# Softmax of the strided heads in batches 0 and 1: one subtraction on VectorE, one exponential, one sum, and batch 1's mask from TensorE

## The chip, the cores and the metric

The kernel runs on one core of a Trainium2 chip. The metric is the device time of one execution in microseconds (us); lower is better. Five engines work side by side, each on its own queue in order: TensorE (PE in the profile; PEld is its weight load), VectorE (DVE), ScalarE (ACT), GpSimd (POOL) and SyncE (SP), which here issues every DMA.

## What is computed

Three stages follow one another: sparse attention, a gated feed-forward, and a soft mixture of experts.

```python
# q, k, v: (4 batches, 8 heads, 576 positions, 64)
scores = scale * np.matmul(q, k.transpose(0, 1, 3, 2))
mask_local = (rel >= 0) & (rel < 32)                             # heads 0 to 3
mask_strided = (rel >= 0) & (pos[None, :] % 32 == pos[:, None] % 32)   # heads 4 to 7
scores = np.where(masks, scores, -1e9)
scores = scores - np.max(scores, axis=-1, keepdims=True)
attn = np.exp(scores)
attn = attn / (np.sum(attn, axis=-1, keepdims=True) + 1e-09)
x = np.matmul(attn, v)                  # then (2304 tokens, 512)
h = x @ w_in                            # 512 -> 2048
x = (h / (1 + np.exp(-1.702 * h))) @ w_out
logits = x @ phi                        # 32 slots; softmax over tokens and over slots,
...                                     # 8 experts on 4 slots each, and the mix back
```

## The kernel before

**Attention.** Heads go in pairs: pairs 0 and 1 are local, pairs 2 and 3 strided. A strided pair has its positions sorted by residue, so its scores become 11 units of 64 query rows x 64 keys (18 positions of each of three residues, hence a block mask). Two heads stand side by side on 128 partitions. The 11 units are split into part 0 (6 units, 384 elements per partition) and part 1 (5 units, 320 elements), each in one PSUM tile `s`. `att_scores` computes them (L176). For batch 0 it first writes the mask into the tile by a bf16 product of the identity `identb` and `maskb` (L166), and the scores accumulate on top. For the other batches VectorE adds the mask later, while it moves the scaled scores from `s` into the SBUF tile `ts` (L192).

**Softmax.** `att_softmax` takes a part at a time. VectorE finds the negated maximum of each unit's rows (L202); in batch 0 it also scales this (L204). ScalarE then runs one exponential per unit (L207): the bias is that unit's negated maximum, and the sum along the row comes out through the accumulator, which shows as a second instruction, ACTIVATION_READ_ACCUMULATOR. VectorE adds 1e-9 and takes the reciprocal (L208, L209). GpSimd multiplies (L210). After that `att_transpose` turns the probabilities on TensorE (L225) and copies them out (L227, L229), and `att_values` multiplies by v (L244) and splits the result into two rounded tiles `x` (L269 on ScalarE, L270 on VectorE).

**The order.** Batch 0 runs alone at the start; `keep_busy` puts filler products on TensorE between its steps (L87). Then the feed-forward runs over five chunks of tokens (c) and sixteen column blocks (f) each; a step (c, f) is one `gemm1`: twelve products (L353), a tanh on ScalarE (L356) and a gate on VectorE (L357). Chunk 0 carries batch 1's attention beside it, chunk 1 batch 2's, chunk 2 batch 3's. Chunk 0 also converts the raw weights: two ScalarE and two VectorE instructions for each block of 512 columns (`narrow`: L286, L287, L288, L289, tiles `wc`, `wt`, `neg`), then a rounded part on ScalarE (L306) and the remainder on GpSimd (L307). The `wt` tiles feed the small products `wp` (L314). The instruction order on each engine is laid out at build time by the framework's planner, from its own estimates of costs; only the last stage is ordered by hand. The PSUM tiles of attention come from a pool of five.

Of the kernel before, what the change touches and what calls it, by code (L numbers as in the profile page):

```python
# [9 lines left out]
F32 = mybir.dt.float32  # L10
# [6 lines left out]
AF = mybir.ActivationFunctionType  # L17
ALU = mybir.AluOpType
AX = mybir.AxisListType
# [12 lines left out]
SCALE = 0.125  # L32
# [16 lines left out]
def tile_kernel(ctx: ExitStack, tc: tile.TileContext, lqk, lv, sqk, sv, wraw, phi, wexp, cst, out):  # L49
    nc = tc.nc  # L50
    P = 128
# [14 lines left out]
    att = att_es.enter_context(tc.tile_pool(name="att", bufs=2, side="right"))  # L66
# [7 lines left out]
    def mtile(name):  # L74
        return ps_m.tile([P, 512], F32, tag="m", name=name)
# [67 lines left out]
    def att_units(hp):  # L143
        local = hp < 2
        return (KL, QT, S, NTL, 5, maskL) if local else (KS, QS, SW, NTS, HS, maskS)

    def att_scores(b, hp, parts=(0, 1)):
        t = qkv[b, hp]
        local = hp < 2
        nk, step, ko, total, half, mask = att_units(hp)  # L150
        early = b == 0
        shape = [P, NTL if local else 2 * HS, nk]
        if (b, hp) not in probs:
            if b == 0 and hp >= 2:
                ts = ep.tile(shape, F32, name=f"ts_{b}_{hp}")
            else:
                ts = att.tile(shape, F32, tag="ts", name=f"ts_{b}_{hp}")
            probs[b, hp] = ts
            if not local:
                nc.gpsimd.memset(ts[:, NTS], 0.0)  # L160
        sp = sps.setdefault((b, hp), {})
        for part in parts:
            nt = (half, total - half)[part]
            sp[part] = (mtile(f"s_{b}_{hp}_{part}")[:, :nt * nk].rearrange("p (u k) -> p u k", k=nk))
            if early:
                nc.tensor.matmul(sp[part], identb, mask.unsqueeze(1).to_broadcast([P, nt, nk]), start=True, stop=False)  # L166
                if local and part == 0:
                    nc.tensor.matmul(sp[0][:, 0], identb, maskL0, start=False, stop=False)
        for u in range(half):
            for part in parts:  # L170
                if part * half + u >= total:
                    continue
                qo = step * (part * half + u)
                for h in range(2):
                    hs, o = slice(64 * h, 64 * h + 64), 64 * (h ^ part)
                    nc.tensor.matmul(sp[part][o:o + 64, u], t[hs, qo:qo + 64], t[hs, ko + qo:ko + qo + nk], start=not early, stop=not early or part * half + u in (half - 1, total - 1))  # L176

    def att_softmax(b, hp, part):
        local = hp < 2
        nk, step, ko, total, half, mask = att_units(hp)  # L180
        u0, u1 = (0, half) if part == 0 else (half, total)
        nt = u1 - u0
        early = b == 0
        nm = f"{b}_{hp}_{part}"
        sp = sps[b, hp][part]
        if local:
            ts = probs[b, hp][:, u0:u1]
        else:
            ts = probs[b, hp].rearrange("p (j e) k -> p e j k", e=2)[:, part, :nt]

        def add_mask(a, z, m):
            nc.vector.scalar_tensor_tensor(ts[:, a:z], sp[:, a:z], SCALE, m.unsqueeze(1).to_broadcast([P, z - a, nk]), op0=ALU.mult, op1=ALU.add)  # L192

        if not early:
            if local and part == 0:
                add_mask(0, 1, maskL0)
                add_mask(1, nt, mask)
            else:
                add_mask(0, nt, mask)
        nmx = att.tile([P, 6], F32, tag="nmx", name=f"nmx_{nm}", bufs=4)  # L200
        src, sc = (sp, SCALE) if early else (ts, 1.0)
        nc.vector.tensor_reduce(nmx[:, :nt], src, axis=AX.X, op=ALU.max, negate=True)  # L202
        if early:
            nc.vector.tensor_scalar_mul(nmx[:, :nt], nmx[:, :nt], SCALE)  # L204
        sm = att.tile([P, 6], F32, tag="sm", name=f"sm_{nm}", bufs=4)
        for u in range(nt):
            nc.scalar.activation(ts[:, u], src[:, u], AF.Exp, scale=sc, bias=nmx[:, u:u + 1], accum_out=sm[:, u:u + 1])  # L207
        nc.vector.tensor_scalar_add(sm[:, :nt], sm[:, :nt], 1e-9)  # L208
        nc.vector.reciprocal(sm[:, :nt], sm[:, :nt])  # L209
        nc.gpsimd.tensor_tensor(ts, ts, sm[:, :nt].unsqueeze(2).to_broadcast([P, nt, nk]), op=ALU.mult)  # L210

    def att_transpose(b, hp):
        ts = probs.pop((b, hp))
# [394 lines left out]
    def attention_units(b):  # L608
        la = 2 if b else 4
        order = list(range(la)) + [x for u in range(la, 8) for x in (la - 1 - u, u)] + list(range(la - 9, -9, -1))  # L610
        for x in order:
            if x >= 0:
                if b and x % 2 == 0:
                    load_qk(b, x // 2)
                att_scores(b, x // 2, (x % 2,))
                att_softmax(b, x // 2, x % 2)
                if b == 0:
                    keep_busy(1)
            else:
                x = -x - 1  # L620
                if x % 2:
                    att_values(b, x // 2)
                else:
                    if b:
                        load_v(b, x // 2)
                    att_transpose(b, x // 2)
                    if (b, x) == (1, 6):
                        load_qk(2, 0)
                if b == 0:
                    keep_busy(4)  # L630
            yield

    def attention_pairs(b):
        for hp in range(4):
            if hp:
                att_values(b, hp - 1)
            att_scores(b, hp)
            att_softmax(b, hp, 0)
            yield
            att_softmax(b, hp, 1)  # L640
            load_v(b, hp)
            if hp < 3:
                load_qk(b, hp + 1)
            yield
            if hp < 3:
                yield
            att_transpose(b, hp)
            yield
        att_values(b, 3)
        if b < 3:  # L650
            load_qk(b + 1, 0)
        yield
# [284 lines left out]
```

## Time and profile before

| | |
|---|---|
| median of 3 runs | 414.33 us (413.97 to 415.26) |
| profiled execution, its own time | 415.33 us |
| its span, first to last instruction | 413.5 us |
| TensorE busy | 387.9 us, 94% |
| VectorE busy | 267.6 us, 65% |
| ScalarE busy | 224.8 us, 54% |
| GpSimd busy | 52.4 us, 13% |
| mean granted TensorE clock | 0.986 |

The shares are means over stages that differ. In the forty slices of the span ScalarE is at 80% or more, mostly over 90%, through much of the first quarter and then falls away, while TensorE is at 90% or more for nearly the whole rest. The first quarter is batch 0's attention and chunk 0 with batch 1's attention, which is where all the changed code runs.

### The profile page before, as it was taken

The numbers are of one execution on the slowest core, as the hardware profiler recorded it, in microseconds if no ns is written. First come the engines' busy times: TensorE is split into PE (matmuls) and PEld (weight loads), VectorE is DVE, ScalarE is ACT, GpSimd is POOL, SyncE is SP. The second block draws the span as 40 slices with busy tenths as digits, with TensorE's granted clock in tenths as the row PEclk, the third lists the DMA queues.
The fourth block names the chain that finished last, engine by engine and source line by source line (L and its number), as shares of the span: only waits on it lengthen the run. The fifth ranks groups of instructions, "written<-read, shape, count | busy, mean of one in ns | idle before, by whom it ended". The sixth has DMA issues, their size and how long they took to land.

```text
span 413.5 us, 9788 instructions
## 1 busy us (share of the span) xinstructions
PE 387.9 (94%) x3930; PEld 269.4 (65%) x3935; DVE 267.6 (65%) x569; ACT 224.8 (54%) x668; POOL 52.4 (13%) x64
## 2 busy tenths in 40 slices
PE   8998998897999999989999999999999999799992
PEld 3656766664776657857767685776778788333682
DVE  2679887799688668868677878547454666412132
ACT  2899789998876546675854758321212222310141
POOL 0433333432310100010110101000000000010000
PEclk9999899999999999999999999999999999999997
DMA  8966477766731422546752442596002899879998
GB/s 237 390 216 212 138 229 238 226 214 229 232 128 43 165 78 98 179 164 211 265 201 78 139 170 101 207 366 268 2 0 103 313 379 334 316 292 406 419 391 259
DMA packets 27917, 89.26 MB, mean 216 GB/s; under 512 B 2400, under 2 KB 9696, under 8 KB 23776
## 3 DMA queue, kind: packets, MB, share of 16 engines
q1 hardware_dynamic: 27872, 88.64, 60.7%
q8 instruction: 31, 0.51, 0.5%
q14 instruction: 14, 0.11, 0.1%
HBM read 79.71 MB, written 8.91 MB: 214 GB/s over the span
## 4 chain that ended last, share of the span: by engine, by line
PE 64%; ACT 16%; DVE 11%; issue 3%; DMA 2%; POOL 2%; SPq 0%; ACTq 0%; DVEq 0%; POOLq 0%
PE h L353 34%; ACT ts L207 7%; PE u L479 5%; PE op L803 4%; PE hp L773 3%; PE lg L372 3%; PE ptp L225 2%; ACT neg L287 2%; PE s L176 2%; PE av L244 2%; DMA qk<-lqk 2%; DVE x L270 2%; PE fp L819 2%; ACT gT L356 2%; DVE wc L289 1%
## 5 line engine op out<-in xcount | busy, mean ns | idle before, releaser
L353 PE MATMUL h<-x,wi 128*128 128x512 f32 (+1 forms) x960 | 217.1, 378 | 2.8 <-DVE gT L357 2.6
L353 PEld LDWEIGHTS h<-x,wi 128*128 128x128 f32 x960 | 165.3, 190 | 52.0 <-issue 14.0
L356 ACT ACTIVATE gT<-h 128x512 f32<-128x512 f32 (+1 forms) x54 | 29.4, 545 | 51.6 <-PE h L353 51.6
L357 DVE SCALAR_TENSOR_TENSOR gT<-gT,h 128x512 f32<-128x512 f32 (+1 forms) x54 | 33.3, 617 | 34.7 <-ACT gT L356 34.3
L207 ACT ACTIVATE ts<-ts,nmx 128x64 f32<-128x64 f32 (+1 forms) x120 | 41.4, 348 | 11.3 <-DVE nmx L202 11.3
L210 POOL TENSOR_TENSOR ts<-ts,sm 128x384 f32<-128x384 f32 (+2 forms) x32 | 27.5, 859 | 156.8 <-DVE sm L209 75.1
L356 ACT ACTIVATE more<-h 128x512 f32<-128x512 f32 (+1 forms) x26 | 14.8, 568 | 40.6 <-PE h L353 40.6
L287 ACT ACTIVATE neg<-raw,ebias 128x512 f32<-128x512 int16 x48 | 36.6, 762 | 0.0
L380 DVE STREAM_TRANSPOSE gT<-gT 128x512 f32<-128x512 f32 (+1 forms) x54 | 34.3, 640 | 1.5 <-PE lg L372 0.3
L307 POOL TENSOR_TENSOR wi<-wc,wi 128x512 fp32r<-128x512 f32 x16 | 22.0, 1374 | 26.0 <-ACT wi L306 17.0
L357 DVE SCALAR_TENSOR_TENSOR more<-more,h 128x512 f32<-128x512 f32 (+1 forms) x26 | 16.9, 651 | 12.6 <-ACT more L356 12.0
L269 ACT CAST x<-av 128x320 fp32r<-128x320 f32 (+20 forms) x54 | 18.9, 400 | 10.9 <-DVE x L270 9.1
L225 PE MATMUL ptp<-cs,ts 128*96 128x128 f32 (+1 forms) x120 | 17.3, 279 | 6.7 <-POOL ts L210 3.7
L479 PE MATMUL u<-gT,dT 32*32 32x512 f32 x576 | 21.4, 597 | 2.0 <-DVE z L537 1.6
L207 ACT ACTIVATION_READ_ACCUMULATOR ts<-ts,nmx 128x1 f32 x120 | 22.5, 188 | 0.0
L270 DVE TENSOR_TENSOR x<-av,x 128x320 fp32r<-128x320 f32 (+20 forms) x54 | 19.9, 394 | 2.6 <-ACT x L269 2.6
L372 PE MATMUL lg<-gT,wp 128*32 128x512 f32 (+1 forms) x100 | 19.9, 566 | 1.1 <-DVE gT L357 1.1
L225 PEld LDWEIGHTS ptp<-cs,ts 128*96 128x96 f32 (+1 forms) x120 | 13.0, 133 | 11.7 <-POOL ts L210 10.5
L176 PEld LDWEIGHTS s<-qk 64*64 64x64 f32 x552 | 15.8, 136 | 5.9 <-issue 4.4
L176 PE MATMUL s<-qk 64*64 64x96 f32 (+1 forms) x552 | 18.9, 240 | 0.6 <-DMA qk<-lqk 0.6
L380 DVE STREAM_TRANSPOSE gT<-more 128x512 f32<-128x512 f32 (+1 forms) x26 | 17.3, 671 | 1.6 <-PE u L479 1.0
L244 PEld LDWEIGHTS av<-pt,v 96*64 96x64 f32 (+2 forms) x552 | 13.9, 136 | 5.8 <-issue 3.5
(154 smaller groups left out, 475.6 us busy)
## 6 DMA issues: line engine op xcount, KB each, us to landing
ex<-wexp SPq DMA_DIRECT2D x28, 1024.0 KB, 7.0
raw<-wraw SPq DMA_DIRECT2D x48, 511.8 KB, 4.0
qk<-lqk SPq DMA_DIRECT2D x8, 592.0 KB, 5.8
wo_scr<-wo SPq DMA_DIRECT2D x16, 256.0 KB, 2.3
ex<-wo_scr SPq DMA_DIRECT2D x4, 1024.0 KB, 9.8
gT<-wexp SPq DMA_DIRECT2D x4, 1024.0 KB, 6.0
qk<-sqk SPq DMA_DIRECT2D x6, 604.0 KB, 5.2
v<-lv SPq DMA_DIRECT2D x8, 432.0 KB, 5.1
```

The source lines that it names most:

```text
L176: nc.tensor.matmul(sp[part][o:o + 64, u], t[hs, qo:qo + 64], t[hs, ko + qo:ko + qo + nk], start=not early, stop=not early or part * half + ...
L207: nc.scalar.activation(ts[:, u], src[:, u], AF.Exp, scale=sc, bias=nmx[:, u:u + 1], accum_out=sm[:, u:u + 1])
L210: nc.gpsimd.tensor_tensor(ts, ts, sm[:, :nt].unsqueeze(2).to_broadcast([P, nt, nk]), op=ALU.mult)
L225: nc.tensor.transpose(ptp[:nk, u - a], src, ident)
L270: nc.vector.tensor_tensor(dsts[1], src, dsts[0].bitcast(F32), op=ALU.subtract)
L287: nc.scalar.activation(n, top, AF.Relu, scale=-(2.0 ** 19), bias=ebias)
L353: nc.tensor.matmul(h[:, :N], w[:, we, 128 * kt:128 * kt + 128], x[xe][:, kt, :N], start=n == 0, stop=n == 11)
L356: st["tanh"] = nc.scalar.activation(g[:, :N], h[:, :N], AF.Tanh, scale=0.851).ins
L357: st["gate"] = nc.vector.scalar_tensor_tensor(g[:, :N], g[:, :N], 1.0, h[:, :N], op0=ALU.add, op1=ALU.mult).ins
L372: nc.tensor.matmul(lgs[c][32 * j:32 * j + 32, :N], wp[:, f0 + j, :], gs[c, f0 + j][:, :N], start=f0 == 0, stop=f0 == NF - 4)
L380: nc.vector.transpose(t_slots(c)[:, f, :N], gs[c, f][:, :N])
L479: nc.tensor.matmul(us[a][32 * j:32 * j + 32, :].rearrange("p (t f) -> p t f", f=32), dT[q, 32 * b:32 * b + 32], gT[q, :, 32 * b:32 * b + 3 ...
```

## The change

For strided pairs of batches 0 and 1 (`joined`), the softmax of a part becomes: the negated maximum of the raw scores on VectorE; one VectorE addition of that maximum to the whole part, from PSUM into `ts`; one exponential with a constant scale over the whole part, in place; one VectorE sum over it. The end (reciprocal, GpSimd's multiplication) is as before, in a helper. For batch 1 the mask of these pairs now comes from TensorE, as in batch 0. Local pairs, and batches 2 and 3, stay as they are.

```diff
@@ att_scores
-        early = b == 0
+        early = b == 0 or b == 1 and not local
@@
+    def softmax_scale(ts, sm, nt, nk):
+        nc.vector.tensor_scalar_add(sm[:, :nt], sm[:, :nt], 1e-9)
+        nc.vector.reciprocal(sm[:, :nt], sm[:, :nt])
+        nc.gpsimd.tensor_tensor(ts, ts, sm[:, :nt].unsqueeze(2).to_broadcast([P, nt, nk]), op=ALU.mult)
@@ att_softmax
+        joined = b < 2 and not local
...
-        if not early:
+        if not early and not joined:
...
+        sm = att.tile([P, 6], F32, tag="sm", name=f"sm_{nm}", bufs=4)
+        if joined:
+            nc.vector.tensor_reduce(nmx[:, :nt], sp, axis=AX.X, op=ALU.max, negate=True)
+            nc.vector.tensor_tensor(ts, sp, nmx[:, :nt].unsqueeze(2).to_broadcast([P, nt, nk]), op=ALU.add)
+            nc.scalar.activation(ts, ts, AF.Exp, scale=SCALE)
+            nc.vector.tensor_reduce(sm[:, :nt], ts, axis=AX.X, op=ALU.add)
+            softmax_scale(ts, sm, nt, nk)
+            return
...
-        sm = att.tile([P, 6], F32, tag="sm", name=f"sm_{nm}", bufs=4)
         for u in range(nt):
             nc.scalar.activation(ts[:, u], src[:, u], AF.Exp, scale=sc, bias=nmx[:, u:u + 1], accum_out=sm[:, u:u + 1])
-        nc.vector.tensor_scalar_add(sm[:, :nt], sm[:, :nt], 1e-9)
-        nc.vector.reciprocal(sm[:, :nt], sm[:, :nt])
-        nc.gpsimd.tensor_tensor(ts, ts, sm[:, :nt].unsqueeze(2).to_broadcast([P, nt, nk]), op=ALU.mult)
+        softmax_scale(ts, sm, nt, nk)
```

## Rows read from the trace of the kernel before

**Rows 1.** Windows of the span: busy us of each engine, its instructions, clock, DMA

```profile
16.00:41.00 25.00, 22.41 (x338) 16.18 (x338) 20.66 (x52) 23.58 (x94) 8.46 (x9) 1.00 0.72 248
66.00:83.00 17.00, 15.21 (x129) 11.00 (x128) 13.20 (x25) 16.11 (x46) 6.39 (x6) 1.00 0.72 226
83.00:104.00 21.00, 18.55 (x149) 11.73 (x146) 20.37 (x36) 19.08 (x52) 5.52 (x6) 0.94 0.63 218
106.00:414.00 308.00, 294.42 (x3026) 205.14 (x3023) 185.49 (x400) 135.90 (x387) 17.30 (x25) 0.99 0.58 210
```

**Rows 2.** Chain of work that ended last, 0 to 112 us: start, us, what

```profile
17.37 1.90 ACT ts L207 x12
...
22.57 1.91 ACT ts L207 x12
...
69.46 1.51 ACT ts L207 x9
...
89.43 1.52 ACT ts L207 x9
```

**Rows 3.** TensorE's waits, 16 to 111 us: total us, times, longest

```profile
PE ptp L225 <- POOL ts L210: 2.6, 4, 1.2
PE h L353 <- DVE gT L357: 2.6, 4, 1.3
PE ptp L225 <- DVE sm L208: 2.2, 1, 2.2
PE wp L314 <- DVE wt L289: 1.9, 2, 1.7
```

**Rows 4.** ScalarE's timeline, batch 0, then batch 1: start, us, what

```profile
17.37 0.32 ACT L207 ACTIVATE ts<-s,nmx 128x64 f32<-128x64 f32 x1
...
19.12 0.35 ACT L269 CAST x<-av 128x192 fp32r<-128x192 f32 x1
...
27.86 0.50 ACT L229 COPY pt<-ptp 128x384 f32<-128x384 f32 x1
28.21 0.81 ACT L287 ACTIVATE neg<-raw,ebias 128x512 f32<-128x512 int16 x1
...
68.89 0.33 ACT L207 ACTIVATE ts<-ts,nmx 128x64 f32<-128x64 f32 x1
...
70.88 0.61 ACT L306 CAST wi<-wc 128x512 fp32r<-128x512 f32 x1
71.39 0.59 ACT L356 ACTIVATE gT<-h 128x512 f32<-128x512 f32 x1
```

**Rows 5.** VectorE's timeline: start, us, what

```profile
85.76 0.55 DVE L192 SCALAR_TENSOR_TENSOR ts<-s,maskb 128x384 f32<-128x384 f32 x1
86.22 1.52 DVE L289 SCALAR_TENSOR_TENSOR wt<-raw,wt 128x512 uint32<-128x512 uint32 x1
...
88.27 0.54 DVE L202 TENSOR_REDUCE nmx<-ts 128x6 f32<-128x384 f32 x1
88.73 0.67 DVE L288 TENSOR_TENSOR wc<-wc,neg 128x512 int32<-128x512 f32 x1
...
95.61 0.48 DVE L202 TENSOR_REDUCE nmx<-ts 128x5 f32<-128x320 f32 x1
96.01 1.78 DVE L289 SCALAR_TENSOR_TENSOR wc<-raw,wc 128x512 uint32<-128x512 uint32 x1
```

**Rows 6.** VectorE's groups by form, 0 to 112 us: busy us, mean ns

```profile
L204 DVE TENSOR_SCALAR nmx<-nmx 128x6 f32<-128x6 f32 x2 | 0.4, 220 | 0.1
```

**Rows 7.** TensorE's timeline around a mask product and two waits

```profile
15.10 0.33 PE L166 MATMUL s<-maskb,identb 128*128 128x384 bf16 x1
15.35 0.92 PE L176 MATMUL s<-qkv 64*64 64x64 f32 x24
...
41.79 0.75 PE L225 MATMUL ptp<-cs,ts 128*96 128x128 f32 x5 [2.24 <-DVE sm L208]
```

**Rows 8.** Windows of 2 us: columns as in the first group

```profile
44.00:46.00 2.00, 2.00 (x22) 1.63 (x21) 1.09 (x2) 2.00 (x4) 0.27 (x2) 0.50 0.06 12
```

## The prediction

> **What bounds the kernel now.** I read the windows of the span first, since the shares of the whole hide the stages [rows 1]. From 106 us on, TensorE is busy 294.4 of 308 us and ScalarE 135.9: that part is TensorE's own, none of the changed instructions lies in it, and what is gained or lost ahead of it should reach the end one for one. The changed code runs in three earlier stretches: 16 to 41 us (batch 0's strided pairs, then the first steps of the feed-forward) and 66 to 83 and 83 to 104 us (batch 1's strided pairs, beside the weight conversion). There the picture is another. ScalarE is busy 23.58 of 25 us, 16.11 of 17 and 19.08 of 21. VectorE stands at 20.66, 13.20 and 20.37 in the same stretches. So ScalarE is the fullest engine in the first two, and VectorE in the third, where it has only 0.63 us left.
>
> Second, the chain of waits [rows 2]. Between 16 and 104 us it runs mostly through ScalarE and VectorE, and the exponentials of the strided parts stand in it: a whole part at 17.37 and at 22.57 us (1.9 us each, twelve instructions), and most of one at 69.46 and 89.43. The reader is to see that a part's six exponentials are not hidden: the next block of weights or the next part stands behind them on ScalarE's queue.
>
> Third, TensorE's waits between 16 and 111 us [rows 3]. They sum to 2.6 + 2.6 + 2.2 + 1.9 = 9.3 us, for probabilities, for the gate, and for converted weights. That is the most that relief of the other engines could give back in this region if nothing else took over. One of them, 2.24 us ahead of 41.79, is the largest single hole [rows 7]; it ends only when the softmax of batch 1's first (local) part is through, which stands behind weight conversion on both engines.
>
> **What the change removes.** Prices are steps in the queue, from the start of the first to the start of what comes next, because consecutive instructions overlap. In batch 0 six exponentials with their accumulator reads take from 17.37 to 19.12, 1.75 us; five take 5/6 of that, 1.46. In batch 1, from SBUF, six take from 68.89 to 70.88, 1.99 us; five take 1.66 [rows 4]. The trace has no exponential over a whole part. The nearest rows bound it: the copy of 384 elements out of PSUM steps 0.35 us (27.86 to 28.21), the rounding of 512 elements in SBUF steps 0.51 (70.88 to 71.39) [rows 4]. I take 0.40 for 384 elements and 0.35 for 320; the ends would shift a part by 0.1 us at most. Each batch has two parts of each size. ScalarE's relief is
>
> - batch 0: 2 x (1.75 - 0.40) + 2 x (1.46 - 0.35) = 4.9 us
> - batch 1: 2 x (1.99 - 0.40) + 2 x (1.66 - 0.35) = 5.8 us
>
> The scaling of the negated maximum in batch 0 goes too: four instructions of some 0.2 us [rows 6], of which the queue feels perhaps 0.12 each, 0.5 us in all.
>
> **What it adds to VectorE.** The sum over a part has the shape of the maximum that is already there: 88.27 to 88.73 is 0.46 us for 384 elements, 95.61 to 96.01 is 0.40 for 320 [rows 5]. The subtraction reads PSUM and a broadcast operand and writes `ts`, as the mask addition does, which steps 0.46 us for 384 elements (85.76 to 86.22) [rows 5]; 320 elements I put at 0.40, as for the sum. The trace has no subtraction with this operand; as it has one PSUM operand of the same size, I see no reason for more than 0.1 us either way. In batch 0 both are new: 2 x (0.46 + 0.46) + 2 x (0.40 + 0.40) = 3.4 us, less the 0.5 above, so +2.9. In batch 1 the subtraction takes the mask addition's place at the same price, and only the sums are new: 2 x 0.46 + 2 x 0.40 = +1.7 us.
>
> **What it adds to TensorE.** Four mask products in batch 1. In batch 0 one of 384 columns steps 0.25 us (15.10 to 15.35) [rows 7]; four, two of them shorter, are at most 1.0 us. Below, they cost nothing where they fall into one of the waits of [rows 3], which is ahead of the scores in some places at best. I count half, 0.5 us.
>
> **What moves.** In batch 0 the PSUM tile `s` comes free after the subtraction instead of after the last exponential, well over 1 us earlier. In batch 1 it is held from the maximum through the subtraction, one more VectorE step than before, about 0.5 us plus what the planner puts between them. No transfer is added or moved. The new waits are the sum's on the exponential, and the exponential's on the subtraction. Behind the sum on VectorE's queue stand weight conversion and gates; the exponential is 0.4 us long, so the wait is short if ScalarE's queue is short, and the accumulator's reader (L208) had the same wait before. GpSimd's multiplication keeps its work. The latency of one part without queues goes from 0.1 + 1.75 (scaled maximum and exponentials, batch 0) to 0.46 + 0.40 + 0.46, some 0.5 us less.
>
> **A price against it.** The sum that ScalarE's accumulator gave inside its own instruction is now a VectorE reduction, 0.46 us in the rows of the same shape [rows 5], in a stretch where VectorE has 0.63 us left [rows 1]. The Trainium skill speaks against that: VectorE: DVE Perf Modes, section Rules for kernel authors, expects a reduction to run at the plain rate only, calls it the slowest VectorE operation, and asks to restructure one that lies on the hot path. By that rule the third stretch would lose what the sums cost; this is the second rival below, and the rows bear it out for that stretch alone.
>
> **The sum by stretches.** 16 to 41 us: ScalarE falls to 23.6 - 4.9 = 18.7 us, VectorE rises to 20.7 + 2.9 = 23.6 of 25. VectorE is next, so at most 1.4 us can go, and TensorE's queue there holds fillers in a fixed order. I take 0.8 us. Bounds: 1.4, and on the other side a loss of 0.5, if VectorE's conversions slip by one subtraction.
>
> 66 to 104 us, taken together since conversion runs steps ahead: ScalarE falls from 35.2 to 29.4, VectorE rises from 33.6 to 35.3, TensorE from 33.8 to at most 34.8, of 38 us. VectorE is again next, at most 38 - 35.3 = 2.7 us can go. VectorE was 88% busy with ScalarE nearly full beside it; if it reaches 95% with ScalarE at ease, the stretch takes 37.2 us, 0.8 less. The chain gives more: it passes 1.5 us and more of exponentials at 69.46 and at 89.43, each of which shrinks to 0.4, 2.2 us together, before VectorE takes over. Between 0.8 and 2.2 I take 1.8, less the 0.5 of mask products: 1.3 us.
>
> Together 2.1 us. The profiled execution took 415.33 us for a span of 413.5, 1.0 above the median of 414.33; the difference is applied to the median: **412.2 us**, 0.5% less. A difference of 0.3%, 1.2 us, is about what can be told from no change.
>
> **The rivals.**
>
> *ScalarE's relief is used up by the next queue* (chance 0.22). Fillers hold TensorE's order in batch 0 and VectorE follows at once. For: VectorE is at 83%, 78% and 97% in the three stretches [rows 1]. Then 0.4 us remains of the 2.1: 413.9, no change that can be told.
>
> *VectorE becomes the bound, and it is slower* (chance 0.17). Place: 83 to 104 us. The two sums of the fourth pair add 0.46 + 0.40 = 0.86 us to 20.37, 21.23 in a stretch of 21; the wait of the `wp` products for converted weights [rows 3] grows by as much, and the pair's mask products add 0.5 us. If the first stretch gives nothing either, the time is 414.3 + 0.9 + 0.5 = 415.7. It decides from the point where VectorE has no idle time left to take the sums, and where ScalarE's relief in 66 to 83 does not let conversion run ahead. Against it: in 66 to 83 VectorE has 3.8 us idle, in which earlier conversion fits.
>
> *The whole chain shrinks* (chance 0.12). Both ceilings are reached, 1.4 + 2.7 = 4.1 us: 410.2. The clock could add to it: at 44 to 46 us TensorE is granted 0.50 of full speed, the 1.2 GHz level [rows 8], after the 2.24 us hole [rows 7]; at full clock the same work would take 1 us less, if the smaller hole left the clock up. I count none of it, and let the low end hold part of it.
>
> *The change doesn't do what it says* I leave out: which instructions are issued is plain from the code; only the planner's new order is open, and it may move any of the above by about 1 us.
>
> **How the numbers follow.** Forecast 0.49 (own range 411.0 to 413.0), used up 0.22, slower 0.17, whole chain 0.12. Faster by over 0.3%: nearly all of the first and the last, 0.58. Within 0.3%: 0.25. Slower: 0.17. The range, 409.7 to 415.4, takes in the low end's 410.2 with half of the clock's 1 us, and reaches up to the slower rival short of its full price; what lies outside is some 0.15.
>
> **What would show it.** Right: ScalarE's busy time 66 to 104 us near 29, eight exponentials of 0.45 to 0.55 us each in place of 44 pairs; VectorE up by 4.6 us in the first 110; the last batch 1 strided probabilities ready before 104 us, and everything after 106 us the same, only earlier. Wrong: VectorE continuously busy from 83 us with a larger wait of `wp` for `wt`; a larger hole near 40 us; a new hole ahead of batch 1's strided scores (PSUM tile not free); or a gain at 106 us that is gone by the end.

## The result and the profile after

The changed kernel takes **410.85 us** (median of 4 runs, 410.67 to 411.28). The kernel before, run beside it on the same chip, takes 414.38 (413.97 to 415.26). The ratio is 0.9913, with an interval of 0.9896 to 0.9931: 3.5 us faster, where 2.1 us were forecast. The profiled execution took 410.86 us, with a span of 409.1. One execution of all those below, of the run with the first seven remainders on VectorE, was in a slow state, and medians and ratios leave it out.

I read the windows first, as before. These rows answer to [rows 1]; the columns are the same, and 66 to 104 us is added in one piece:

```profile
16.00:41.00 25.00, 22.05 (x331) 15.90 (x325) 23.81 (x57) 20.45 (x54) 10.14 (x9) 1.00 0.77 253
...
66.00:83.00 17.00, 17.00 (x134) 11.89 (x131) 16.75 (x30) 16.25 (x32) 9.11 (x7) 1.00 0.69 247
83.00:104.00 21.00, 19.07 (x162) 13.20 (x156) 21.00 (x39) 17.46 (x32) 7.47 (x7) 1.00 0.73 248
106.00:409.00 303.00, 289.89 (x3000) 201.57 (x2989) 183.24 (x396) 132.66 (x381) 16.03 (x24) 0.99 0.58 210
...
66.00:104.00 38.00, 36.07 (x293) 25.09 (x287) 37.75 (x68) 33.72 (x63) 16.58 (x13) 1.00 0.72 248
```

The same row of the kernel before, which the prediction formed as a sum of two:

```profile
66.00:104.00 38.00, 33.76 (x274) 22.73 (x270) 33.57 (x61) 35.20 (x97) 11.91 (x11) 0.97 0.67 221
```

The roles have changed sides. In 66 to 104 us VectorE is now the full engine, 37.75 of 38 us. ScalarE has 34 instructions fewer but is only 1.5 us less busy. Replacing 44 exponentials and accumulator reads by 4 leaves 57 of its 97 instructions; the profile shows 63, so six others have moved into the stretch from later on: four of the weight conversion, a tanh and a copy of `wpT`. TensorE does 2.3 us more in it.

The new instructions by form, 0 to 112 us (busy us, mean ns of one, idle time ahead), with the mask products' group that now holds batch 1's too:

```profile
L210 DVE TENSOR_TENSOR ts<-s,nmx 128x384 f32<-128x384 f32 x4 | 2.2, 550 | 0.0
L212 DVE TENSOR_REDUCE sm<-ts 128x6 f32<-128x384 f32 x4 | 2.2, 546 | 0.4 <-ACT x L280 0.4
L211 ACT ACTIVATE ts<-ts 128x384 f32<-128x384 f32 x4 | 2.1, 519 | 0.6 <-DVE ts L210 0.6
L166 PE MATMUL s<-maskb,identb 128*128 128x384 bf16 x6 | 2.0, 330 | 0.0
...
L212 DVE TENSOR_REDUCE sm<-ts 128x5 f32<-128x320 f32 x4 | 1.9, 482 | 0.1
L210 DVE TENSOR_TENSOR ts<-s,nmx 128x320 f32<-128x320 f32 x4 | 1.9, 480 | 0.0
L211 ACT ACTIVATE ts<-ts 128x320 f32<-128x320 f32 x4 | 1.9, 473 | 0.3 <-DVE ts L210 0.3
```

TensorE's waits, 16 to 111 us, which answer to [rows 3]:

```profile
PE ptp L236 <- DVE sm L179: 3.4, 1, 3.4
PE ptp L236 <- POOL ts L181: 3.3, 4, 1.3
PE h L364 <- DVE gT L368: 1.0, 1, 1.0
PE h L364 <- ACT wt L297: 0.2, 1, 0.2
```

They sum to 7.9 us instead of 9.3. The wait of `wp` for converted weights is gone and the gate's has shrunk from 2.6 to 1.0, but the single hole near 40 us [rows 7] has grown from 2.24 to 3.44.

To see where the time went, I took four points of TensorE's timeline that every run has: the start of batch 1's first strided scores, of its last strided scores, of batch 2's first scores, and the end. Up to batch 1's first strided scores both kernels need the same (65.23 and 65.22 us), and up to its last ones too (91.46 and 91.60). From there to batch 2's first scores it is 23.47 us before and 19.52 after. From there to the end of the span it is 298.6 and 298.0. Of the 4.4 us between the two spans, 3.95 arise in the 20 us behind the last strided scores, where feed-forward and weight conversion finish.

### The profile page after: what moved, and what is told of

It reads as the page before. It is cut to its first block, busy times and chain, and to the rows that moved or that the text cites. A ratio compares the mean times of both kernels' runs of the same rounds, so it can differ in the third digit from the quotient of the medians.

```text
span 409.1 us, 9725 instructions
## 1 busy us (share of the span) xinstructions
PE 385.8 (94%) x3939; PEld 269.3 (66%) x3939; DVE 272.5 (67%) x577; ACT 215.7 (53%) x588; POOL 55.1 (13%) x64
## 4 chain that ended last, share of the span: by engine, by line
PE 64%; DVE 16%; ACT 11%; issue 4%; DMA 2%; POOL 2%; SPq 0%; DVEq 0%; ACTq 0%; POOLq 0%
PE h L364 33%; ACT ts L220 5%; PE u L490 5%; PE op L814 4%; PE hp L784 3%; PE lg L383 3%; PE av L255 3%; PE s L176 3%; PE ptp L236 2%; DVE x L281 2%; DVE gT L368 2%; DMA qk<-lqk 2%; PE fp L830 2%; POOL ts L181 1%; DVE wc L300 1%
## 5 line engine op out<-in xcount | busy, mean ns | idle before, releaser
L368 DVE SCALAR_TENSOR_TENSOR gT<-gT,h 128x512 f32<-128x512 f32 (+1 forms) x54 | 33.2, 616 | 31.8 <-ACT gT L367 31.4
L181 POOL TENSOR_TENSOR ts<-ts,sm 128x384 f32<-128x384 f32 (+2 forms) x32 | 29.7, 929 | 148.4 <-DVE sm L180 73.1
L220 ACT ACTIVATE ts<-ts,nmx 128x96 f32<-128x96 f32 (+1 forms) x98 | 34.2, 352 | 12.4 <-DVE nmx L216 12.4
L318 POOL TENSOR_TENSOR wi<-wc,wi 128x512 fp32r<-128x512 f32 x16 | 22.2, 1388 | 26.4 <-ACT wi L317 26.2
L236 PE MATMUL ptp<-cs,ts 128*96 128x128 f32 (+1 forms) x120 | 17.4, 282 | 8.6 <-POOL ts L181 4.9
L368 DVE SCALAR_TENSOR_TENSOR more<-more,h 128x512 f32<-128x512 f32 (+1 forms) x26 | 16.9, 648 | 12.1 <-ACT more L367 11.5
L236 PEld LDWEIGHTS ptp<-cs,ts 128*96 128x96 f32 (+1 forms) x120 | 13.3, 134 | 14.2 <-POOL ts L181 13.2
L383 PE MATMUL lg<-gT,wp 128*32 128x512 f32 (+1 forms) x100 | 20.9, 566 | 0.8 <-DVE gT L368 0.8
L220 ACT ACTIVATION_READ_ACCUMULATOR ts<-ts,nmx 128x1 f32 x98 | 18.5, 189 | 0.0
L240 ACT COPY pt<-ptp 96x384 f32<-96x384 f32 (+1 forms) x34 | 14.7, 478 | 5.7 <-PE ptp L236 5.6
```

The costliest lines, as they stand in the source:

```text
L236: nc.tensor.transpose(ptp[:nk, u - a], src, ident)
L368: st["gate"] = nc.vector.scalar_tensor_tensor(g[:, :N], g[:, :N], 1.0, h[:, :N], op0=ALU.add, op1=ALU.mult).ins
L383: nc.tensor.matmul(lgs[c][32 * j:32 * j + 32, :N], wp[:, f0 + j, :], gs[c, f0 + j][:, :N], start=f0 == 0, stop=f0 == NF - 4)
```

## The experiments

Each diff is against the changed kernel. Each ratio is against the kernel before on the same chip (its medians there were 414.77 to 415.12, and 414.38 for the first row of the changed kernel). The stretches are A, span start to batch 1's first strided scores; B, to its last strided scores; C, to batch 2's first scores; each is a difference of starts in TensorE's timeline. They come from the one profiled execution of each run, which lies up to 1.2 us from its run's median and 2.2 us above it for the extra copy, so they don't add up to the differences of the medians.

| run | ratio (interval) | A | B | C |
|---|---|---|---|---|
| kernel before | 1 | 65.2 | 26.2 | 23.5 |
| changed kernel | 0.9913 (0.9896 to 0.9931) | 65.2 | 26.4 | 19.5 |
| batch 0 only | 0.9977 (0.9959 to 0.9995) | 64.5 | 25.9 | 23.5 |
| batch 1 only | 0.9967 (0.9953 to 0.9981) | 65.5 | 25.0 | 22.7 |
| mask move alone | 0.9958 (0.9938 to 0.9978) | 64.4 | 26.6 | 22.7 |
| two sums | 0.9940 (0.9919 to 0.9961) | 65.8 | 26.2 | 20.1 |
| changed kernel again | 0.9909 (0.9876 to 0.9942) | 64.3 | 26.4 | 19.6 |
| extra copy | 1.0013 (0.9984 to 1.0041) | 65.6 | 27.5 | 22.6 |
| fillers | 0.9942 (0.9921 to 0.9962) | 66.3 | 24.5 | 19.9 |
| all remainders on VectorE | 0.9918 (0.9891 to 0.9945) | 61.3 | 26.3 | 24.6 |
| first seven on VectorE | 0.9880 (0.9849 to 0.9911) | 60.9 | 27.1 | 22.8 |
| batch 1 only, last three on VectorE | 0.9969 (0.9953 to 0.9984) | 65.5 | 25.0 | 22.0 |
| batch 1 only, first seven on VectorE | 0.9867 (0.9840 to 0.9894) | 62.6 | 26.3 | 19.4 |
| batch 1 only, last three left out | 0.9912 (0.9884 to 0.9939) | 64.9 | 25.1 | 20.6 |

Stretch A also varies with the landing of the first loads: batch 0's first scores start between 6.3 and 7.5 us.

**The halves.** Batch 0 joined alone, then batch 1 alone:

```diff
-        early = b == 0 or b == 1 and not local
+        early = b == 0
...
-        joined = b < 2 and not local
+        joined = b == 0 and not local
```

> Only batch 0's strided pairs are joined; batch 1 as in the kernel before. Theory A (batch 1 carries the whole gain; in batch 0 VectorE took over and the hole near 40 us grew from 2.24 to 3.44 us): 414.0 to 415.2 us, no change or a little slower, with VectorE at about 23.8 of 25 us between 16 and 41 us. Theory B (the prediction's split, 0.8 us from batch 0): 413.0 to 413.8.

```diff
-        joined = b < 2 and not local
+        joined = b == 1 and not local
```

> Only batch 1's strided pairs are joined, with the mask from TensorE; batch 0 as before. Theory A: 410.0 to 411.2 us, the whole gain or more, with TensorE's hole near 40 us back at about 2.2 us. Theory B: 411.6 to 413.0, since batch 0's share is missing. If neither half alone gives the gain, it comes from the planner's order of the two together (theory C).

Batch 0 alone took 414.13 us, 0.23% less than before; batch 1 alone 413.61, 0.33% less. The halves add up to 0.56%; the whole gives 0.87%. By these ratios alone the difference is hardly outside the noise, since their intervals reach 0.14 to 0.18% either way. Stretch C says it more plainly: it is 0.0 and 0.7 us shorter with the halves, and 3.9 us with the whole and with its repetition. So something in stretch C hangs on both. Batch 1 alone has VectorE's work of 66 to 104 us (36.87 us busy, 33.82 for ScalarE, nearly those of the whole change) and yet loses most of C's gain. VectorE's timeline of that run ahead of the gate (L368), for which TensorE waits:

```profile
98.54 0.49 DVE L209 TENSOR_REDUCE nmx<-s 128x5 f32<-128x320 f32 x1
98.94 1.39 DVE L300 SCALAR_TENSOR_TENSOR wc<-raw,wc 128x512 uint32<-128x512 uint32 x1
100.26 0.68 DVE L299 TENSOR_TENSOR wt<-wt,neg 128x512 int32<-128x512 f32 x1
100.86 0.48 DVE L210 TENSOR_TENSOR ts<-s,nmx 128x320 f32<-128x320 f32 x1
101.26 1.63 DVE L300 SCALAR_TENSOR_TENSOR wt<-raw,wt 128x512 uint32<-128x512 uint32 x1
102.81 0.68 DVE L368 SCALAR_TENSOR_TENSOR gT<-gT,h 128x512 f32<-128x512 f32 x1
```

GpSimd's timeline of the same run:

```profile
97.93 1.86 POOL L318 TENSOR_TENSOR wi<-wc,wi 128x512 fp32r<-128x512 f32 x1 [2.89 <-DVE x L281]
101.06 1.28 POOL L318 TENSOR_TENSOR wi<-wc,wi 128x512 fp32r<-128x512 f32 x1 [1.28 <-ACT wi L317]
```

TensorE's timeline shows what follows:

```profile
103.54 2.56 PE L364 MATMUL h<-x,wi 128*128 128x512 f32 x10 [2.79 <-DVE gT L368]
```

The same six instructions of VectorE in the changed kernel:

```profile
97.43 0.48 DVE L209 TENSOR_REDUCE nmx<-s 128x5 f32<-128x320 f32 x1
97.83 0.68 DVE L300 SCALAR_TENSOR_TENSOR wc<-raw,wc 128x512 uint32<-128x512 uint32 x1
98.43 0.68 DVE L299 TENSOR_TENSOR wt<-wt,neg 128x512 int32<-128x512 f32 x1
99.03 0.48 DVE L210 TENSOR_TENSOR ts<-s,nmx 128x320 f32<-128x320 f32 x1
99.43 0.67 DVE L300 SCALAR_TENSOR_TENSOR wt<-raw,wt 128x512 uint32<-128x512 uint32 x1
100.03 0.67 DVE L368 SCALAR_TENSOR_TENSOR gT<-gT,h 128x512 f32<-128x512 f32 x1
```

From the maximum to the gate it is 2.60 us here and 4.27 us with batch 1 alone. The instructions are the same; two conversions (L300, L289 in the kernel before) take 1.39 and 1.63 us instead of 0.68, each beside one of GpSimd's remainders (L318); such a pair is called a meeting below. In the changed kernel the remainders of this time lie at 95.67 and 100.26 us, mostly beside other instructions. That became the theory for the rest: where GpSimd's two-input instructions fall decides what VectorE's conversions cost, and so what stretch C takes.

**The mask move alone.** The exponentials stay single in both batches, batch 1's mask comes from TensorE (both lines in `att_softmax`):

```diff
-        early = b == 0
-        joined = b < 2 and not local
+        early = b == 0 or b == 1 and not local
+        joined = False
```

> Batch 1's strided mask comes from TensorE, but the exponentials stay one per unit with bias and accumulator, in both batches; nothing is joined. VectorE then does a tiny scaling (0.1 us) in place of a mask addition (0.46), so it is relieved by about 1.4 us, ScalarE's exponentials from PSUM step 0.29 in place of 0.33 us, TensorE gets four mask products. Theory A (ScalarE's queue was what held the conversion back): 413.6 to 415.0, little changed. Rival (VectorE's relief and the mask products make the gain): 411 to 412.5.

Measured: 413.41 us, 0.42% less than before, a little faster than theory A said, and short of the rival. Four mask additions leave VectorE, tiny scalings take their place, and TensorE's four products cost no time that shows. The mask move alone thus gives as much as batch 1 joined with it (0.33%): in this order of instructions, joining batch 1 alone adds nothing to it.

**Two sums.** Is VectorE the bound now? Batch 1's four sums are formed twice:

```diff
             nc.vector.tensor_reduce(sm[:, :nt], ts, axis=AX.X, op=ALU.add)
+            if b:
+                extra = att.tile([P, 6], F32, tag="extra", name=f"extra_{nm}", bufs=2)
+                nc.vector.tensor_reduce(extra[:, :nt], ts, axis=AX.X, op=ALU.add)
```

> The changed kernel with each of batch 1's four sums done twice (the second into a tile nobody reads): 1.7 us more on VectorE between 66 and 104 us. If VectorE is now the bound of that stretch (it is busy 37.75 of 38 us): 1.2 to 2.0 us slower than the changed kernel, 412.0 to 412.9. If its idle time elsewhere hides them: under 0.5 us, 410.8 to 411.3.

Measured: 412.55 us, 1.1 to 1.7 us over the two medians of the changed kernel (411.43 and 410.85), for 2 x 0.46 + 2 x 0.40 = 1.7 us of added queue steps. So by the medians most of VectorE's added time counts, as the theory of a full VectorE expects. The profiled executions don't place the loss there: B and C together, where the sums stand, take 46.3 us against 45.9, and the rest of the difference lies in A and behind C, where nothing was added. In 66 to 104 us conversions longer than 0.95 us take 3.9 us more than 0.68 each would, against 5.3 in the changed kernel, which may hide 1.4 of the 1.7 us there. The run is in line with VectorE as the bound, and doesn't show it by itself.

**The changed kernel again**, as a control beside the next three:

> The changed kernel once more, unaltered, as the yardstick for the other three runs on the same chip: a ratio of 0.989 to 0.993 to the kernel before.

Measured: 411.43 us, ratio 0.9909. The result repeats.

**An extra copy on ScalarE.** Does ScalarE have room now?

```diff
+            if b:
+                nc.scalar.copy(ts, ts)
             nc.vector.tensor_reduce(sm[:, :nt], ts, axis=AX.X, op=ALU.add)
```

> The changed kernel with an in-place ScalarE copy of the whole part after each of batch 1's four exponentials: about 1.6 us more on ScalarE, 0.4 us more latency of each part, nothing on VectorE. Theory A (ScalarE has slack between 66 and 104 us now): at most 0.5 us slower than the changed kernel, clearly less than the 1.7 us of second sums cost. If ScalarE still bounds: 1.2 to 2 us slower.

Measured: 415.98 us, 4.6 us over its control, for four copies of 0.44 to 0.53 us. This was a miss. The copies lie in the chain from exponential to sum, and with them the order around them changed. The profiled execution took 418.15 us, 7.8 more than that of the control: 1.3 us in A, 1.1 in B, 3.0 in C and 2.4 behind C, the first and the last of which no copy touches. In C a conversion meets GpSimd's remainder of 102.34 us, ahead of the gate (VectorE's timeline):

```profile
102.53 1.63 DVE L302 SCALAR_TENSOR_TENSOR wt<-raw,wt 128x512 uint32<-128x512 uint32 x1
104.09 0.68 DVE L370 SCALAR_TENSOR_TENSOR gT<-gT,h 128x512 f32<-128x512 f32 x1
```

and TensorE's next block of products, behind a hole of 1.96 us, runs at 0.50 of the clock (its timeline; 13 products in 4.83 us, where 12 take 2.96 in the changed kernel):

```profile
104.82 4.83 PE L366 MATMUL h<-x,wi 128*128 128x512 f32 x13 [1.96 <-DVE gT L370]
```

So this run doesn't price ScalarE's room alone. How much of the 4.6 us is the longer chain, how much the new order and how much the clock stays open.

**Fillers in the hole near 40 us.** Twelve small products are put in line ahead of batch 1's first transposition, to keep TensorE busy through the hole:

```diff
+                    if (b, x) == (1, 0):
+                        keep_busy(12, mtile("fill"))
```

> The changed kernel with twelve filler products of 512 columns (2.6 us) on TensorE ahead of batch 1's first transposes, where TensorE waits 3.4 us and then runs at the 1.2 GHz level from 44 to 50 us. If the low clock costs time there: the granted clock between 44 and 50 us goes from about 0.5 to 1.0 and the kernel gets 1 to 2.5 us faster than the changed one. If VectorE and ScalarE set the pace there anyway: the clock rises and the time stays within 0.5 us.

Measured: 412.55 us, 1.1 us over its control. The planner put the fillers at 36.04 us, ahead of other products and not into the hole, which was still 3.04 us. The run tells nothing of what the hole's clock costs.

**All remainders on VectorE.** The 16 weight remainders that GpSimd subtracted go to VectorE, so that none of them can meet a conversion:

```diff
-        nc.gpsimd.tensor_tensor(w[:, 1], t, w[:, 0].bitcast(F32), op=ALU.subtract)
+        nc.vector.tensor_tensor(w[:, 1], t, w[:, 0].bitcast(F32), op=ALU.subtract)
```

> The changed kernel with the sixteen remainders of the weight split on VectorE in place of GpSimd: 16 x 0.60 = 9.6 us more on VectorE's list, but GpSimd no longer works beside VectorE's conversions, some of which take 1.1 to 1.8 us instead of 0.68 while it does. Theory A with collisions (about 0.7 us lost for each GpSimd instruction that meets one): about even, 409.8 to 412 us, with all of VectorE's conversions outside the four strided parts near 0.68 us. If the long conversions have another cause, the 9.6 us come on top and the kernel is 4 us or more slower.

Measured: 411.91 us, 0.5 us over its control. Within the intervals that is no difference. Stretch A is 3 us shorter than in its control, with a hole near 40 us of only 0.74 us; C is 5 us longer, with new holes of 2.63 and 2.89 us and 0.50 of the clock from 101.08 us on. VectorE now has a step of some 0.6 us more to do for each late block; that this makes the holes is argued from its queue. The remedy helps early and not late.

**The first seven on VectorE**, in the changed kernel:

```diff
+        (nc.vector if f < 7 else nc.gpsimd).tensor_tensor(w[:, 1], t, w[:, 0].bitcast(F32), op=ALU.subtract)
```

> The changed kernel with the remainders of the first seven weight blocks on VectorE, the other nine on GpSimd. With all sixteen on VectorE the early part up to batch 1's first strided scores came 4 us sooner, and the late part lost it again in three waits of 2.2 to 2.9 us. If the two parts are independent: the early gain stays and the late part is that of the changed kernel, 407.5 to 409.5 us, ratio 0.982 to 0.988. If the late part is lost again whatever stands before it: 410.5 to 412.

Measured: 409.80 us, 0.9880: a little better than the changed kernel (0.9909 and 0.9913), within the intervals. In the profiled execution (410.89 us) A gains 3.4 us on the changed kernel's second run; B and C, 0.8 and 3.2 longer, give it back. In C TensorE hardly waits longer than there (2.2 us against 2.1), but behind a hole of 1.53 us it was granted 0.50 from 102.04 to about 109 us, and the same work took it 3.1 us more. The two executions with a mean clock of 0.993 and 0.994 took 408.11 and 409.04 us, so the late loss isn't the remedy's price alone.

**Batch 1 only, with the last three on VectorE** (`joined` for batch 1, and `f >= 13` in the line above): if the late meetings cost batch 1 alone its gain, taking them away should bring it back.

> Only batch 1 joined, and the last three remainders (the ones that met VectorE's conversions between 93 and 102 us) on VectorE. Theory D: batch 1 alone fell short of the whole change because its conversions met GpSimd there (1.3 to 1.8 us each in place of 0.68) and the gate came late, so TensorE waited 2.8 us: that wait is under 1.5 us now, and the kernel is at 0.989 to 0.993 of the kernel before, as the whole change. Theory B (batch 0's relief of ScalarE is really needed): it stays at 0.996 to 0.998.

Measured: 413.84 us, no different from batch 1 alone (413.61). The long conversions between 97 and 103 us are gone (0.67 to 0.69 us each), but the remainders that stand in VectorE's queue instead cost most of what was saved: the gate starts at 102.08 instead of 102.81, and TensorE still waits 2.05 us for it. The test was not clean.

**Batch 1 only, with the first seven on VectorE** (`f < 7`): the early remedy without batch 0's join.

> Only batch 1 joined, and the first seven remainders on VectorE. If joining batch 0 earns nothing by itself: as fast as the same with batch 0 joined (e9), within 0.3%. If batch 0's part matters: 1 us or more slower than e9.

Measured: **409.10 us**, 0.9867 (0.9840 to 0.9894), the best of all. It beats the kernel before by 1.3%. The changed kernel took 410.85 us with 0.9896 to 0.9931, and 411.43 with 0.9876 to 0.9942, on other occasions; beside the same runs of the kernel before, the changed kernel with the same early remedy took 409.80. Its window of 44 to 46 us, and then its TensorE timeline:

```profile
44.00:46.00 2.00, 1.73 (x25) 1.43 (x26) 1.52 (x4) 1.38 (x3) 0.37 (x2) 1.00 0.53 207
```
```profile
41.71 0.75 PE L236 MATMUL ptp<-cs,ts 128*96 128x128 f32 x5 [1.74 <-POOL ts L181]
```

The hole is 1.74 us and the clock stays at 1.00, where the kernel before was granted 0.50 [rows 8]. With this split, batch 0's join isn't needed for the gain (0.9867 against 0.9880). The early split without any join was not run, so how much of the 1.3% is the join's stays open.

**Batch 1 only, with the last three remainders left out.** The clean test: GpSimd writes zeros instead (at 75.08 us and from 84.56 on, earlier than the remainders stood) and reads nothing, VectorE gets nothing to do, and the order on VectorE, ScalarE and TensorE is that of batch 1 alone.

```diff
-        nc.gpsimd.tensor_tensor(w[:, 1], t, w[:, 0].bitcast(F32), op=ALU.subtract)
+        nc.gpsimd.memset(w[:, 1].bitcast(F32), 0.0) if f >= 13 else nc.gpsimd.tensor_tensor(w[:, 1], t, w[:, 0].bitcast(F32), op=ALU.subtract)
```

> As the kernel with only batch 1 joined, but the last three weight remainders are left out (GpSimd fills those three tiles with zeros instead, reading nothing); every instruction of VectorE, ScalarE and TensorE stands in the same order as there. Theory D (batch 1 alone fell short because its conversions met GpSimd between 93 and 102 us): the conversions there are back at 0.68 us, the gate that came at 102.8 us comes 1.5 us or more sooner, TensorE's wait of 2.8 us ahead of it falls under 1.4, and the kernel is at a ratio of 0.990 to 0.994 to the kernel before in place of 0.9967. Theory B (batch 0's relief of ScalarE is needed for the rest): the wait and the ratio stay, 0.995 to 0.998.

Measured: 411.00 us, 0.9912, against 0.9967 with the remainders. The gate comes 2.9 us sooner, TensorE's wait for it falls from 2.79 to 1.40 us, and C from 22.7 to 20.6. VectorE's timeline ahead of the gate:

```profile
97.37 0.68 DVE L300 SCALAR_TENSOR_TENSOR wc<-raw,wc 128x512 uint32<-128x512 uint32 x1
...
99.27 0.68 DVE L300 SCALAR_TENSOR_TENSOR wt<-raw,wt 128x512 uint32<-128x512 uint32 x1
99.87 0.68 DVE L368 SCALAR_TENSOR_TENSOR gT<-gT,h 128x512 f32<-128x512 f32 x1
```

Batch 1 alone has three conversions that these remainders stretch, 1.79 us at 93.80, 1.39 and 1.63, together 2.8 us above 0.68 each (GpSimd's remainders start at 93.29, 97.93 and 101.06); without them the median is 2.6 us lower, 2.3 by the ratios. The theory holds: those meetings are the difference between batch 1 alone and a gain as large as the whole change's. Nothing else that the zeros change carries it: no product of `h` waited for a remainder in batch 1 alone, and C's 48 products of `h` keep TensorE busy for 12.1 and 12.2 us. It is the place of the meetings that counts: over the first 112 us the changed kernel has more conversions above 0.95 us than the kernel before (13 and 11), but behind 91.5 us it has two, of 1.79 and 1.07, the second behind the gate that TensorE waits for, where batch 1 alone has four.

## Why the prediction was right, and where it was off

**Prices.** The prices of single instructions held. A whole exponential takes 0.52 and 0.47 us (forecast 0.45 to 0.55), the sum and the subtraction 0.55 and 0.48, like the maximum that they were read from [rows 5]. In the queue, the exponential at 68.68 us is followed at 69.09, a step of 0.41, where 0.40 was taken. The four mask products step 0.24 to 0.27 us each. By the Trainium skill, VectorE: DVE Perf Modes, section Rules for kernel authors, a reduction is VectorE's slowest operation; here it is not: the sum over 384 elements (546 ns) costs what the subtraction of that size costs (550 ns). Its advice against one on the hot path is in line with the doubled sums, which made the kernel 1.1 to 1.7 us slower; the change as a whole was faster all the same.

**16 to 41 us, forecast a gain of 0.8 us.** This step failed: it gave nothing. VectorE rose from 20.66 to 23.81, as priced; ScalarE fell from 23.58 to 20.45, not to 18.7. The hole's end moved from 41.79 to 42.30 us, 0.5 later, which is the step's bad bound; up to batch 1's first strided scores that was made up. VectorE and GpSimd there (two timelines of the changed kernel):

```profile
37.56 1.63 DVE L300 SCALAR_TENSOR_TENSOR wc<-raw,wc 128x512 uint32<-128x512 uint32 x1
39.12 0.54 DVE L216 TENSOR_REDUCE nmx<-ts 128x4 f32<-128x384 f32 x1
...
41.27 1.00 DVE L179 TENSOR_SCALAR sm<-sm 128x4 f32<-128x4 f32 x1 [0.18 <-ACT ts L220]
```
```profile
37.35 1.29 POOL L318 TENSOR_TENSOR wi<-wc,wi 128x512 fp32r<-128x512 f32 x1 [2.44 <-ACT wi L317]
...
41.25 0.99 POOL L181 TENSOR_TENSOR ts<-ts,sm 128x480 f32<-128x480 f32 x1 [2.60 <-ACT ts L220]
```

A conversion beside GpSimd took 1.63 us just ahead of the maximum for which the softmax waits. The bad bound had allowed for conversions that slip by one subtraction; what the timeline shows ahead of the hole's end is this meeting, and a tiny addition (of 1e-9, L179) of 1.00 us beside GpSimd's multiplication where the kernel before had 0.67. The maximum comes 0.51 us later than in the kernel before (38.61), as the hole's end does. No run took this one meeting away by itself. Over the runs whose first stretch has neither fillers nor another split of the remainders, A is the same with batch 0 joined (65.2, 64.5, 65.8, 64.3 and 65.6 us: mean 65.1) and without it (65.2, 65.5, 64.4, 65.5 and 64.9: mean 65.1). Batch 0's part of the change buys nothing up to there.

The clock moved the wrong way too: behind the longer hole the low level lasted longer than in the kernel before, which was granted 0.84, 0.50, 0.81 and 1.00 in the same windows (of 2 us, the second in [rows 8]):

```profile
42.00:44.00 2.00, 1.25 (x8) 0.98 (x9) 1.97 (x5) 0.68 (x3) 1.07 (x2) 0.77 0.79 254
44.00:46.00 2.00, 2.00 (x21) 1.64 (x21) 0.27 (x1) 1.84 (x4) 0.15 (x1) 0.50 0.26 94
46.00:48.00 2.00, 2.00 (x10) 1.49 (x7) 1.53 (x4) 1.71 (x4) 1.01 (x1) 0.50 0.00 0
48.00:50.00 2.00, 2.00 (x6) 1.52 (x6) 1.68 (x3) 1.78 (x10) 0.26 (x1) 0.53 0.00 0
```

**66 to 104 us, forecast a gain of 1.3 us.** The direction was right and the term was too small: stretch C measured 3.95 us less. That the whole came out near the forecast is partly luck, since the first term was 0.8 us too large and this one more than 2 us too small. VectorE did become the fullest engine, as the sum said it would, but the kernel wasn't slower for it: with ScalarE at ease, VectorE's work ran ahead into 66 to 83 us (13.20 to 16.75 of 17). The ceiling of 2.7 us counted idle time only, inside that window, and what changed in C is more than idle time. TensorE's timeline splits C at the first transposition of the last strided probabilities (`ptp`, L225 before, L236 after), and shows how many of C's 48 products of `h` are left behind it:

| run | last strided scores to transposition | from there to batch 2's first scores | products of `h` left |
|---|---|---|---|
| kernel before | 14.0 us | 9.5 us | 24 |
| changed kernel | 12.5 | 7.1 | 14 |
| batch 0 only | 14.0 | 9.5 | 24 |
| mask move alone | 13.2 | 9.5 | 24 |
| batch 1 only | 15.7 | 7.1 | 14 |
| batch 1 only, last three left out | 13.5 | 7.1 | 14 |

So 2.4 of the 3.95 us are ten products that the planner's order puts ahead of the transposition when batch 1 is joined, and 1.5 us are a shorter way to the probabilities. Batch 1 alone has the ten products too, but a longer way, 2.2 us of which go without its three late meetings. Two things that TensorE met ahead of the transposition are gone. In the kernel before, the wait of 1.75 us for `wt` ahead of 99.53 stands behind a conversion of 1.78 us at 96.01 [rows 5], beside a remainder of GpSimd at 95.94: a meeting that the changed kernel doesn't have ahead of these products. And behind that hole the kernel before ran at a low clock (a window of it, then its TensorE timeline):

```profile
100.00:106.00 6.00, 5.69 (x19) 3.85 (x18) 5.01 (x12) 5.65 (x18) 1.97 (x2) 0.72 0.69 239
```
```profile
92.19 1.05 PE L314 MATMUL wp<-wt,phs 128*32 128x512 f32 x4
93.41 1.05 PE L314 MATMUL wp<-wt,phs 128*32 128x512 f32 x2 [0.18 <-DVE wt L289]
...
99.53 1.04 PE L314 MATMUL wp<-wt,phs 128*32 128x512 f32 x2 [1.75 <-DVE wt L289]
100.81 4.58 PE L353 MATMUL h<-x,wi 128*128 128x512 f32 x12 [0.24 <-DVE gT L357]
105.47 0.87 PE L225 MATMUL ptp<-cs,ts 128*128 128x128 f32 x6
```

The changed kernel's TensorE timeline has the same twelve products at the full clock:

```profile
92.33 3.04 PE L364 MATMUL h<-x,wi 128*128 128x512 f32 x12
95.29 1.23 PE L325 MATMUL wp<-wt,phs 128*32 128x512 f32 x8
96.77 2.96 PE L364 MATMUL h<-x,wi 128*128 128x512 f32 x12 [0.25 <-ACT wt L297]
...
104.07 0.87 PE L236 MATMUL ptp<-cs,ts 128*128 128x128 f32 x6 [0.73 <-POOL ts L181]
```

Their 4.58 us became 2.96, 1.6 us; the eight `wp` products, which came in three pieces behind waits and partly ahead of the first `h` block, run in one, 1.23 us in place of 3.14, and the second `h` block starts 5.17 us after the last strided scores instead of 9.35. Of C's 3.95 us, TensorE's own account is 1.9 us for `wp`, 1.7 for the products of `h`, 0.5 less waiting, and 0.2 more for the rest. That the clock gave its part back isn't shown: batch 0 alone had 1.00 granted in 100 to 106 us and still took 23.5 us for C, with 1.6 us less for the products of `h` and 1.6 us more of waiting, most of it for GpSimd's multiplication. Nor were those executions of the kernel before faster that had a mean clock of 0.990 or more: medians of 415.1 and 414.9 us in two series of 27, against 414.9 and 414.8 for those with 0.985 and 0.986.

**The rivals.** *Used up by the next queue* is what happened in the first stretch, and not in the second. *VectorE becomes the bound, and it is slower* had its condition (21.00 of 21 us in 83 to 104) but not its result, since conversion ran ahead in 66 to 83 us, the point named against it; batch 1 alone comes nearest to it, with the 2.79 us hole. *The whole chain shrinks* gave 410.2, near in size, but by gains in both stretches, which isn't what happened. Of the marks set for a right forecast, ScalarE near 29 us in 66 to 104 failed (33.72), because earlier conversion refilled it. VectorE rose by 8.2 us in the first 110, not by 4.6, with conversion that ran ahead and stretched instructions on top. The last strided probabilities are ready at 104.02 us, at the mark of 104, where the kernel before had 105.41, and from batch 2's first scores on all is as before, within 0.6 us. Of the marks set for a wrong one, the larger hole near 40 us came; VectorE without a pause from 83 us came too, but without the larger wait of `wp`.

**What stays open.** What makes batch 0's join, which gives nothing up to 91 us, improve C when batch 1 is joined too (15.7 us to the transposition without it, 12.5 with it) is shown only as the place of GpSimd's instructions: why the whole change puts GpSimd's late instructions beside gate and sum, and batch 1 alone beside conversions, isn't known; that it is the accident of the planner's order is argued, not shown. The meetings were taken away for batch 1 alone, not for the whole change: what part of its 1.5 us on the way to the probabilities is theirs, and what the clock is worth there, these runs don't tell.

## What to carry to other kernels

When two engines are nearly full in a stretch, relief of one shows the other; look then at who shares with that other one, for its price can more than double by what runs beside it (0.68 to 1.8 us here), without a wait in any view. Try the halves of such a change alone: here one half (batch 0) was not needed, and the other with seven early remainders moved from GpSimd to VectorE was better than the whole. A change's idle-time ceiling holds for its window only: work that moves ahead of a late chain gains outside it. Whether a low clock behind a hole costs anything has to be tried: batch 0 alone got the full clock in C and no time.

## What the runs showed of the hardware

VectorE's conversions with two inputs in SBUF take 0.68 us alone and up to 1.8 us while a two-input instruction of GpSimd runs; GpSimd's remainder takes 1.28 us alone and up to 1.86 (once 2.97, in the run with the first seven on VectorE, beside three conversions of 0.68). Not stretched were VectorE's instructions with one operand in PSUM (in the changed kernel the subtraction of 384 elements, 0.54 us at 86.44 beside the remainder of 86.49, and the gate, 0.67 at 100.03, most of which runs beside that of 100.26) and its reductions (sum of 320 elements, 0.47 at 100.63). A tiny addition to 4 elements took 0.16 us alone and 1.00 us at 41.27, beside a multiplication of GpSimd. GpSimd's write of zeros left a conversion beside it at 0.67 (75.30 us, with the last three left out). The Trainium skill, SBUF — State Buffer, section Who interferes with whom, says this in a rule: a VectorE instruction with two SBUF inputs contends with a GpSimd instruction that reads SBUF, not with one that only writes, and a reduction never contends. The runs agree on each of these points; the tiny addition is none of these cases.

TensorE's low level (0.50, 1.2 GHz) followed holes of 1.96, 2.24, 3.04 and 3.44 us in these runs, in the kernel before one of 1.75, and one of 1.53 us in the changed kernel with the first seven on VectorE; it did not follow holes of 1.74 and 1.79, nor one of 1.75 with the mask move alone, nor the one of 2.79 us in batch 1 alone. Nor did it follow the one of 2.05 us with batch 1 only and the last three on VectorE. The length of the hole alone doesn't tell whether the clock falls.
